# Column sums of phi(k) by a DMA transpose, a VectorE sum and a broadcast read of a DRAM row, in place of a matmul with ones

## Chip, cores and metric

One core of a Trainium2 chip. The metric is the device time of one execution in microseconds. The kernel before takes 213.39 us (median of 6 runs, 212.61 to 214.76).

## The reference, cut to what matters

A linear-attention block and a SwiGLU block on the same normed input, added to the residual. S = 2048 rows, D = 512, 32 heads of 16, F = 1792.

```python
pq, pk = phi(q), phi(k)
kv = jnp.einsum("bhsd,bhse->bhde", pk, v)
z = jnp.einsum("bhsd->bhd", pk)                      # the column sums: 512 numbers
num = jnp.einsum("bhqd,bhde->bhqe", pq, kv)
den = jnp.einsum("bhqd,bhd->bhq", pq, z)[..., None] + 1e-6
o = num / den
...
return x + _A_ref(xn, A_wqkv, A_wo) + _B_ref(xn, B_w_gate, B_w_up, B_w_down)
```

Only z is in question: pk summed over all 2048 rows, then needed in every partition, since den multiplies it by pq row by row.

## The kernel before

Rows lie on partitions. GpSimd and VectorE add the 16 tiles of pk into two accumulators; zb is their sum, 128 partitions x 512. What is left is a sum over the 128 partitions whose result must stand in all of them. A matmul with a matrix of ones does both at once.

```python
NGU = NCH * NFC                                       # 56 gate/up blocks, j = 0..55
O_SLOT = {4: 0, 7: 1, 10: 2, 13: 3}                   # block of a group of 14 -> output tile
PZ_AT = {9 + 11 * t // 4: t for t in range(16)}       # block after which tile t is multiplied by z
DIV_AT = {j + 1: t for j, t in PZ_AT.items()}         # one block later it is divided
...
        def z_bf():      # VectorE
            zb = zacc[0] + zacc[1]
        def z_mm():
            K.add("pe", lambda e: e.matmul(banks[3][:, :], ones[:, :], zb[:, :], start=True, stop=True), ...)
            K.add("act", lambda e: e.activation(zbc[:, :], banks[3][:, :], ACT.Copy), ...)
        def pz_mul(t):   # GpSimd: pz = pq[t] * zbc
        def divide(t):   # VectorE: den = sum over 16 of pz; reciprocal; pq[t] *= 1/den; then a DMA transpose of pq[t]
...
        for j in range(NGU):
            gu(j)        # TensorE: 4 gate and 4 up matmuls of 128x512, banks 4..7 in turn; ScalarE: silu of the gate
            hop(j)       # VectorE: hT = up * silu(gate); frees the up bank for block j + 2
            ...
            if j in DIV_AT: divide(DIV_AT[j])
            if j in PZ_AT:  pz_mul(PZ_AT[j])
            if C >= 1 and fc in O_SLOT: otile(4 * (C - 1) + O_SLOT[fc])
```

(Shortened, with cuts at "...".) VectorE runs its instructions in program order; on VectorE the divide of a tile stands between the hops of two blocks; and the up matmuls of block j + 2 write the bank that hop(j) frees.

Of the kernel before, what the change touches and what calls it, by code (L numbers as in the profile page):

```python
# [6 lines left out]
ACT = mybir.ActivationFunctionType  # L7
ALU = mybir.AluOpType

P = 128  # L10
S = 2048
D = 512
# [3 lines left out]
NG = D // P  # L16
# [6 lines left out]

CENTRED = (0, 1)
NWARM = 8
O_SLOT = {4: 0, 7: 1, 10: 2, 13: 3}
PZ_AT = {9 + 11 * t // 4: t for t in range(16)}
DIV_AT = {j + 1: t for j, t in PZ_AT.items()}


# [77 lines left out]
def bass_parallel_sum__linear_attn_block__swiglu_ffn__prompt_kernel(nc, A_x, A_wqkv, A_wo, B_x, B_w_gate, B_w_up, B_w_down, out):  # L108
    xin = A_x[0]
    oview = out[0]  # L110
    K = _Program()
    bf, f32 = dt.bfloat16, dt.float32

    with contextlib.ExitStack() as es:
        E = es.enter_context

        def sb(name, shape, dtype):
            return E(nc.sbuf_tensor(name, shape, dtype))
# [20 lines left out]
        zb = sb("zb", [P, D], bf)  # L139
# [4 lines left out]
        zbc = sb("zbc", [P, D], f32)  # L144
# [3 lines left out]
        sil = sb("sil", [P, 2, 512], bf)  # L148
        out_sb = sb("out_sb", [P, 2, D], bf)
        ident = sb("ident", [P, P], bf)  # L150
        ones = sb("ones", [P, P], bf)
        maskt = sb("maskt", [P, P], bf)
        eps5 = sb("eps5", [P, 1], f32)
        stats = sb("stats", [P, NT, 6], f32)
# [16 lines left out]
        banks = [E(nc.psum_tensor("pb%d" % i, [P, 512], f32)) for i in range(8)]  # L171

        def B(i):
            return ("bank", i)
# [48 lines left out]
        for t in range(4, 16):  # L223
# [5 lines left out]
            out=ident[:, :], in_=ident[:, :], compare_op=ALU.not_equal, fill=1.0,  # L229
            base=0, pattern=[[-1, P]], channel_multiplier=1), r=[("ident",)], w=[("ident",)])  # L230

        def blockmask(key, ap, view, pat):
            K.add("pool", lambda e: e.memset(ap, 1.0), w=[key])
            K.add("pool", lambda e: e.affine_select(
                out=view, in_=view, compare_op=ALU.is_ge, fill=0.0, base=0,
                pattern=[[-DH, HPG]] + pat, channel_multiplier=1), r=[key], w=[key])
            K.add("pool", lambda e: e.affine_select(
                out=view, in_=view, compare_op=ALU.is_ge, fill=0.0, base=DH - 1,
                pattern=[[DH, HPG]] + pat, channel_multiplier=-1), r=[key], w=[key])

        blockmask(("maskt",), maskt[:, :], maskt[:, :].rearrange("p (a b) -> p a b", a=HPG), [[0, DH]])
        K.add("pool", lambda e: e.memset(ones[:, :], 1.0), w=[("ones",)])

        def keep_busy(k, n):
            one = nc.const_aps.tensor(1.0, (P, 512), bf)
# [200 lines left out]
        def z_add(half, i):  # L446
            acc, key = zacc[:, half, :], ("zacc", half)
            t = NZP * half + i
            if half == 0 and i == 1:
                K.add("pool", lambda e: e.tensor_scalar(  # L450
                    out=acc, in0=pk[:, 0, :], scalar1=rstd[:, 0:1], scalar2=0.0, op0=ALU.mult, op1=ALU.add),
                    r=[("pk", 0), ("rs", 0)], w=[key])
                K.add("pool", lambda e: e.tensor_scalar(
                    out=zt, in0=pk[:, 1, :], scalar1=rstd[:, 1:2], scalar2=0.0, op0=ALU.mult, op1=ALU.add),
                    r=[("pk", 1), ("rs", 1)], w=[("pz", 0)])
                K.add("pool", lambda e: e.tensor_tensor(out=acc, in0=acc, in1=zt, op=ALU.add),
                      r=[key, ("pz", 0)], w=[key])
                return
            first, fkey = (pk[:, t - 1, :], ("pk", t - 1)) if i == 1 else (acc, key)
            K.add("dve" if half else "pool",  # L460
                  lambda e: e.tensor_tensor(out=acc, in0=first, in1=pk[:, t, :], op=ALU.add),  # L461
                  r=[fkey, ("pk", t)], w=[key])
# [50 lines left out]
        def gu(j, extra=(), er=(), ew=()):  # L513
            C, fc = j // NFC, j % NFC
            n = (len(extra) + 7) // 8
            todo = list(extra)
            for b, w_, key in ((gb(j), wg, "wg"), (gb(j) + 1, wu, "wu")):
                fns = []
                for c in range(NDC):
                    fns.append(lambda e, c=c, b=b, w_=w_: e.matmul(  # L520
                        banks[b][:, :], w_[:, c, fc * P:(fc + 1) * P], xnT[:, c, C * 512:(C + 1) * 512],
                        start=(c == 0), stop=(c == NDC - 1)))
                    fns += todo[:n]
                    todo = todo[n:]
                K.add("pe", fns,
                      r=sum([xkeys(t) for t in range(4 * C, 4 * C + 4)], []) + [(key, fc // 7)] + list(er),
                      w=[B(b)] + list(ew))
            K.add("act", lambda e: e.activation(sil[:, j % 2, :], banks[gb(j)][:, :], ACT.Silu),  # L528
                  r=[B(gb(j))], w=[("sil", j % 2)])

        def hop(j):
            C, fc = j // NFC, j % NFC
            K.add("dve", lambda e: e.tensor_tensor(  # L533
                out=hT[:, C % 2, fc, :], in0=banks[gb(j) + 1][:, :], in1=sil[:, j % 2, :], op=ALU.mult),
                r=[B(gb(j) + 1), ("sil", j % 2)], w=[("hT", C % 2, fc)] + (shared.get((C, fc), []) if C < 2 else []))
# [8 lines left out]
        def kv_fns():  # L544
            return [(lambda e, c=c, g=g: e.matmul(  # L545
                banks[0][:, g * P:(g + 1) * P], wqkv[:, c, 2 * D + g * P:2 * D + (g + 1) * P],
                GT[:, c, g * P:(g + 1) * P], start=(c == 0), stop=(c == NDC - 1)))
                for g in range(NG) for c in range(NDC)]

        def kv_mask():  # L550
            K.add("dve", lambda e: e.tensor_tensor(
                out=kvT[:, :, :], in0=banks[0][:, :].rearrange("p (g e) -> p g e", g=NG),
                in1=maskt[:, :][:, None, :].broadcast_to([P, NG, P]), op=ALU.mult),
                r=[B(0), ("maskt",)], w=[("kvT",)])

        def z_bf():
            K.add("dve", lambda e: e.tensor_tensor(out=zb[:, :], in0=zacc[:, 0, :], in1=zacc[:, 1, :], op=ALU.add),
                  r=[("zacc", 0), ("zacc", 1)], w=[("zb",)])

        def z_mm():  # L560
            K.add("pe", lambda e: e.matmul(banks[3][:, :], ones[:, :], zb[:, :], start=True, stop=True),
                  r=[("zb",), ("ones",)], w=[B(3)])
            K.add("act", lambda e: e.activation(zbc[:, :], banks[3][:, :], ACT.Copy), r=[B(3)], w=[("zbc",)])

        def heads(ap):
            return ap.rearrange("p (h d) -> p h d", d=DH)
# [2 lines left out]
        def pz_mul(t):  # L569
            K.add("pool", lambda e: e.tensor_tensor(out=pz[:, t % 2, :], in0=pq[:, t, :], in1=zbc[:, :], op=ALU.mult),  # L570
                  r=[("pq", t), ("zbc",)], w=[("pz", t % 2)])
# [25 lines left out]
        def m_mm(g):  # L597
            K.add("pe", lambda e: e.matmul(banks[MB[g]][:, :], kvT[:, g, :], wo[:, g, :], start=True, stop=True),  # L598
                  r=[("kvT",), ("wo", 0)], w=[B(MB[g])])
            K.add("act", lambda e: e.activation(M[:, g, :], banks[MB[g]][:, :], ACT.Copy), r=[B(MB[g])], w=[("M", g)])  # L600
# [19 lines left out]
        def otile(t):  # L620
            b = t % 4
            ogroup(b, t, 0, D)
            oout(b, t, 0, D)
# [7 lines left out]
        for j in range(NGU):  # L631
            C, fc = j // NFC, j % NFC
            if j == 2:
                gu(j, kv_fns(), [("GT", c) for c in range(NDC)] + [("wqkv", 2, 0)], [B(0)])
            else:
                gu(j)
            hop(j)
            if j == 1:
                z_add(1, 1)
            elif j == 2:  # L640
                kv_mask()
                z_add(1, 2)
            elif j == 3:
                z_add(1, 3)
            elif j == 4:
                m_mm(0)
                m_mm(1)
                z_add(1, 4)
            elif j == 5:
                m_mm(2)  # L650
                m_mm(3)
                z_add(1, 5)
            elif j == 6:
                z_bf()
            elif j == 8:
                z_mm()
            if j in DIV_AT:
                divide(DIV_AT[j])
            if j in PZ_AT:
                pz_mul(PZ_AT[j])  # L660
            if C >= 1 and fc in O_SLOT:
                otile(4 * (C - 1) + O_SLOT[fc])
        for t in range(12, 15):
# [42 lines left out]
```

## Time and profile before

| | before |
|---|---|
| time, median of 6 | 213.39 us |
| span of the profiled execution | 211.8 us |
| TensorE busy | 208.0 us |
| TensorE waiting for another engine after 60 us | 0.2 us of weight load |

### The profile page before, as it was taken

What the parts mean: (1) busy time and instruction counts of PE and PEld (TensorE: products, weight loads), DVE (VectorE), ACT (ScalarE), POOL (GpSimd) and SP (SyncE); (2) the same over time, 40 slices, a digit from 0 to 9 for tenths busy, and PEclk for the clock granted to TensorE, in tenths of its full rate; (3) what the DMA queues carried; (4) which work ended last, traced back from release to release, by engine and by line L of the source; (5) the groups of instructions that cost most, each with busy time, mean ns of one, the idle gap of its engine ahead of it and who ended that gap; (6) DMA issues with size and microseconds to landing.
All of it is one profiled execution on the core that took longest, in us unless ns stands there. A gap on an engine that the chain in (4) does not pass through costs nothing.

```text
span 211.8 us, 2736 instructions
## 1 busy us (share of the span) xinstructions
PE 208.0 (98%) x1009; PEld 95.7 (45%) x1009; DVE 129.2 (61%) x224; ACT 70.3 (33%) x146; POOL 62.9 (30%) x92
## 2 busy tenths in 40 slices
PE   8899899999999999999999999999999999999996
PEld 2344344444544444444444444444444444444455
DVE  3898988973864788654654775564639463542122
ACT  4989886406364333122131313021223122130000
POOL 3879877899402322210201220220204000000000
PEclk9999999999999999999999999999999999999999
DMA  6954731399920021102101011101011101100101
GB/s 177 353 139 101 72 73 35 63 387 370 357 88 0 3 50 25 50 0 53 25 25 25 25 29 50 25 25 50 8 44 26 50 7 46 25 25 0 49 25 53
DMA packets 27997, 16.04 MB, mean 76 GB/s; under 512 B 17872, under 2 KB 27984, under 8 KB 27984
## 3 DMA queue, kind: packets, MB, share of 16 engines
q1 hardware_dynamic: 27152, 15.15, 26.3%
q10 hardware_dynamic: 832, 0.72, 1.1%
q8 instruction: 8, 0.13, 0.3%
q14 instruction: 5, 0.04, 0.1%
HBM read 9.70 MB, written 2.10 MB: 56 GB/s over the span
## 4 chain that ended last, share of the span: by engine, by line
PE 90%; DVE 4%; DMA 3%; POOL 1%; SPq 1%; ACT 1%; issue 0%
PE pb L520 46%; PE pb L608 23%; PE pb L389 7%; PE pb L604 7%; PE pb L438 6%; DMA x_sb<-in_A_x_dram 3%; DVE pk L428 1%; SPq L178 1%; DVE pq L428 1%; DVE stats L256 1%; POOL ef L417 1%; ACT ef L410 1%; PE pb L545 0%; PE pb L598 0%; POOL xn L344 0%
## 5 line engine op out<-in xcount | busy, mean ns | idle before, releaser
L528 ACT ACTIVATE sil<-pb 128x512 bf16<-128x512 f32 x56 | 33.3, 597 | 101.2 <-PE pb L520 98.8
L533 DVE TENSOR_TENSOR hT<-pb,sil 128x512 bf16<-128x512 f32 x56 | 38.1, 687 | 36.7 <-PE pb L520 33.8
L520 PE MATMUL pb<-xnT,wg 128*128 128x512 bf16 x224 | 57.8, 379 | 0.0
L520 PE MATMUL pb<-xnT,wu 128*128 128x512 bf16 x224 | 57.8, 379 | 0.0
L608 PE MATMUL pb<-wd,hT 128*128 128x512 bf16 (+2 forms) x252 | 51.4, 355 | 0.0
L570 POOL TENSOR_TENSOR pz<-pq,zbc 128x512 f32<-128x512 bf16 x16 | 18.6, 1163 | 90.5 <-DVE den L575 78.5
L608 PEld LDWEIGHTS pb<-wd,hT 128*128 128x128 bf16 x252 | 23.5, 98 | 25.0
L520 PEld LDWEIGHTS pb<-xnT,wu 128*128 128x128 bf16 x224 | 21.9, 98 | 25.9 <-DVE hT L533 0.2
L520 PEld LDWEIGHTS pb<-xnT,wg 128*128 128x128 bf16 x224 | 21.9, 98 | 25.8
L614 DVE TENSOR_TENSOR out_sb<-pb,x_sb 128x512 bf16<-128x512 f32 (+2 forms) x18 | 11.4, 632 | 33.2 <-PE pb L608 33.2
L389 PE MATMUL pb<-wqkv,xnT 128*128 128x512 bf16 x112 | 25.2, 379 | 0.8 <-DVE pq L428 0.6
L587 DVE TENSOR_TENSOR pq<-pq,rden 128x512 bf16<-128x512 bf16 x16 | 17.5, 1094 | 0.6
L389 PEld LDWEIGHTS pb<-wqkv,xnT 128*128 128x128 bf16 x112 | 10.8, 98 | 14.5 <-DVE pq L428 1.4
L417 POOL TENSOR_SCALAR ef<-ef 128x512 bf16<-128x512 bf16 x25 | 15.8, 634 | 5.0 <-ACT ef L410 4.5
L604 PE MATMUL pb<-M,pk 128*128 128x512 bf16 (+2 forms) x72 | 16.8, 355 | 0.0
L410 ACT ACTIVATE ef<-pb 128x512 bf16<-128x512 f32 x25 | 14.7, 591 | 3.8 <-PE pb L389 3.8
L256 DVE BATCH_NORM_STATS2 stats<-x_sb 128x6 f32<-128x512 bf16 x16 | 10.9, 679 | 3.6 <-DMA x_sb<-in_A_x_dram 3.6
L438 PE MATMUL pb<-pk,xn 128*128 128x512 bf16 x56 | 12.7, 379 | 0.0
L575 DVE TENSOR_REDUCE den<-pz 128x32 f32<-128x512 f32 x16 | 10.8, 675 | 0.0
L428 DVE SCALAR_TENSOR_TENSOR pk<-pb,ef 128x512 bf16<-128x512 f32 x14 | 9.6, 685 | 1.8 <-POOL ef L417 1.6
L461 POOL TENSOR_TENSOR zacc<-zacc,pk 128x512 f32<-128x512 f32 x8 | 10.2, 1279 | 0.6
L604 PEld LDWEIGHTS pb<-M,pk 128*128 128x128 bf16 x72 | 6.8, 98 | 7.4
(77 smaller groups left out, 109.8 us busy)
## 6 DMA issues: line engine op xcount, KB each, us to landing
out_dram<-out_sb SPq DMA_DIRECT2D x15, 128.0 KB, 1.7
x_sb<-in_A_x_dram SPq DMA_DIRECT2D x14, 128.0 KB, 4.5
wg<-in_B_w_gate_dram SPq DMA_DIRECT2D x2, 896.0 KB, 8.3
wu<-in_B_w_up_dram SPq DMA_DIRECT2D x2, 896.0 KB, 9.7
wd<-in_B_w_down_dram SPq DMA_DIRECT2D x2, 896.0 KB, 13.9
wqkv<-in_A_wqkv_dram ACTq DMA_DIRECT2D x2, 256.0 KB, 4.7
wqkv<-in_A_wqkv_dram SPq DMA_DIRECT2D x2, 256.0 KB, 5.0
wqkv<-in_A_wqkv_dram SPq DMA_DIRECT2D x1, 512.0 KB, 7.8
```

The source lines that it names most:

```text
L389: K.add("pe", [(lambda e, c=c: e.matmul(banks[b][:, :], src[:, c, t * P:(t + 1) * P], wqkv[:, c, col:col + D], start=(c == 0), stop=(c == ...
L410: K.add("act", lambda e: e.activation(buf, banks[b][:, :], ACT.Exp), r=[B(b)], w=[bkey])
L417: K.add("pool", lambda e: e.tensor_scalar(out=buf, in0=buf, scalar1=top, scalar2=0.0, op0=ALU.min, op1=ALU.max), r=[bkey] + tkeys, w=[bkey])
L428: K.add("dve", lambda e: e.scalar_tensor_tensor(out=dst, in0=val, scalar=low, in1=mid, op0=ALU.max, op1=ALU.add), r=keys + lkeys, w=[dkey])
L438: K.add("pe", [(lambda e, c=c: e.matmul(banks[c][:, :], src[:, t, c * P:(c + 1) * P], pk[:, t, :], start=first, stop=last)) for c in range ...
L520: fns.append(lambda e, c=c, b=b, w_=w_: e.matmul(banks[b][:, :], w_[:, c, fc * P:(fc + 1) * P], xnT[:, c, C * 512:(C + 1) * 512], start=(c ...
L528: K.add("act", lambda e: e.activation(sil[:, j % 2, :], banks[gb(j)][:, :], ACT.Silu), r=[B(gb(j))], w=[("sil", j % 2)])
L533: K.add("dve", lambda e: e.tensor_tensor(out=hT[:, C % 2, fc, :], in0=banks[gb(j) + 1][:, :], in1=sil[:, j % 2, :], op=ALU.mult), r=[B(gb( ...
L570: K.add("pool", lambda e: e.tensor_tensor(out=pz[:, t % 2, :], in0=pq[:, t, :], in1=zbc[:, :], op=ALU.mult), r=[("pq", t), ("zbc",)], w=[( ...
L587: K.add("dve", lambda e: e.tensor_tensor(out=heads(pq[:, t, :]), in0=heads(pq[:, t, :]), in1=rden[:, i, :][:, :, None].broadcast_to([P, NH ...
L604: fns = [(lambda e, g=g: e.matmul(banks[bank][:, 0:hi - lo], pk[:, t, g * P:(g + 1) * P], M[:, g, lo:hi], start=(g == 0), stop=False)) for ...
L608: fns = [(lambda e, fc=fc: e.matmul(banks[bank][:, 0:hi - lo], hT[:, C % 2, fc, jj * P:(jj + 1) * P], wd[:, fc, lo:hi], start=False, stop= ...
```

## The change

Its intent is to take the sum off TensorE and PSUM: the DMA engine turns zb so that columns lie on partitions, VectorE sums along the free dimension, and the 512 sums go through a row in DRAM, which is read back into all partitions. As the way is longer, the multiplies and divides start three blocks later and three of four output tiles one block later.

```diff
-O_SLOT = {4: 0, 7: 1, 10: 2, 13: 3}
-PZ_AT = {9 + 11 * t // 4: t for t in range(16)}
+O_SLOT = {5: 0, 8: 1, 11: 2, 13: 3}
+PZ_AT = {12 + 11 * t // 4: t for t in range(16)}
...
+        zrow = nc.dram_tensor("zrow", [1, D], f32, kind="Internal").ap()
...
-        def z_mm():
-            K.add("pe", lambda e: e.matmul(banks[3][:, :], ones[:, :], zb[:, :], start=True, stop=True), ...
-            K.add("act", lambda e: e.activation(zbc[:, :], banks[3][:, :], ACT.Copy), ...
+        def z_turn():      # after z_bf, block 6
+            K.add("sp", lambda e: e.dma_start_transpose(out=zT[:, :, :], in_=zb[:, :]), ...
+        def z_sum():       # block 8
+            K.add("dve", lambda e: e.tensor_reduce(
+                out=zc[:, :], in_=zT[:, :, :], axis=mybir.AxisListType.X, op=ALU.add), ...
+            K.add("sp", lambda e: e.dma_start(zrow[0].rearrange("(g p) -> p g", g=NG), zc[:, :],
+                                            allow_slow_non_contiguous=True), ...
+            K.add("sp", lambda e: e.dma_start(zbc[:, :], zrow.broadcast_to([P, D])), ...
```

(The memset of ones goes too; operand lists are cut.)

More of the change, by code (lines that the diff above doesn't have):

```diff
@@ L150, in bass_parallel_sum__linear_attn_block__swiglu_ffn__prompt_kernel @@
         ident = sb("ident", [P, P], bf)
-        ones = sb("ones", [P, P], bf)
+        zT = sb("zT", [P, NG, P], bf)
+        zc = sb("zc", [P, NG], f32)
+        zrow = nc.dram_tensor("zrow", [1, D], f32, kind="Internal").ap()
         maskt = sb("maskt", [P, P], bf)
@@ L241, in bass_parallel_sum__linear_attn_block__swiglu_ffn__prompt_kernel @@
         blockmask(("maskt",), maskt[:, :], maskt[:, :].rearrange("p (a b) -> p a b", a=HPG), [[0, DH]])
-        K.add("pool", lambda e: e.memset(ones[:, :], 1.0), w=[("ones",)])
         def keep_busy(k, n):
@@ L558, in z_bf @@
                   r=[("zacc", 0), ("zacc", 1)], w=[("zb",)])
-        def z_mm():
-            K.add("pe", lambda e: e.matmul(banks[3][:, :], ones[:, :], zb[:, :], start=True, stop=True),
-                  r=[("zb",), ("ones",)], w=[B(3)])
-            K.add("act", lambda e: e.activation(zbc[:, :], banks[3][:, :], ACT.Copy), r=[B(3)], w=[("zbc",)])
+        def z_turn():
+            K.add("sp", lambda e: e.dma_start_transpose(out=zT[:, :, :], in_=zb[:, :]), r=[("zb",)], w=[("zT",)], dma=True)
+        def z_sum():
+            K.add("dve", lambda e: e.tensor_reduce(
+                out=zc[:, :], in_=zT[:, :, :], axis=mybir.AxisListType.X, op=ALU.add), r=[("zT",)], w=[("zc",)])
+            K.add("sp", lambda e: e.dma_start(zrow[0].rearrange("(g p) -> p g", g=NG), zc[:, :],
+                                            allow_slow_non_contiguous=True),
+                  r=[("zc",)], w=[("zrow",)], dma=True)
+            K.add("sp", lambda e: e.dma_start(zbc[:, :], zrow.broadcast_to([P, D])),
+                  r=[("zrow",)], w=[("zbc",)], dma=True)
         def heads(ap):
@@ L654, in bass_parallel_sum__linear_attn_block__swiglu_ffn__prompt_kernel @@
                 z_bf()
+                z_turn()
             elif j == 8:
-                z_mm()
+                z_sum()
             if j in DIV_AT:
```

## The prediction

> **What bounds the kernel now.** I read the page first, then the chain of waits in order of time, the list of waits, and the timeline around the sum.
>
> The busy shares and the chain, from the page:
>
> ```profile
> PE 208.0 (98%) x1009; PEld 95.7 (45%) x1009; DVE 129.2 (61%) x224; ACT 70.3 (33%) x146; POOL 62.9 (30%) x92
> ...
> PE 90%; DVE 4%; DMA 3%; POOL 1%; SPq 1%; ACT 1%; issue 0%
> PE pb L520 46%; PE pb L608 23%; PE pb L389 7%; PE pb L604 7%; PE pb L438 6%; DMA x_sb<-in_A_x_dram 3%; DVE pk L428 1%; SPq L178 1%; DVE pq L428 1%; DVE stats L256 1%; POOL ef L417 1%; ACT ef L410 1%; PE pb L545 0%; PE pb L598 0%; POOL xn L344 0%
> ```
>
> TensorE is the bound: 90% of the span lies on its instructions in the chain. In order of time the chain stays on TensorE without a break from 25.60 to 210.02 us, so from there on only two things move the end: matmul work put in or taken out, and a wait that stops TensorE. The piece that the change takes out stands in that chain:
>
> ```profile
> 61.19 5.18 PE pb L520 x24
> 66.37 0.22 PE pb L561
> 66.58 17.27 PE pb L520 x80
> 83.85 0.86 PE pb L604 x4
> ```
>
> So the matmul with ones (L561) is worth 0.22 us of the path, and between it and the first output tile at 83.85 us TensorE only does gate and up matmuls, which do not need the sum.
>
> The waits from 60 us on show who is close to TensorE and who is not:
>
> ```profile
> POOL pz L570 <- DVE den L575: 78.5, 14, 7.9
> POOL pz L570 <- ACT zbc L563: 12.0, 1, 12.0
> ...
> PEld pb L520 <- DVE hT L533: 0.2, 1, 0.2
> ```
>
> GpSimd, the consumer of the broadcast row zbc, is idle most of the time. The only wait of TensorE is 0.2 us of weight load on VectorE's hop (the product that frees an up bank). This matters: VectorE runs in order, and where it stands still the hop comes late and TensorE stops two blocks later.
>
> VectorE's timeline where the row is made and first used:
>
> ```profile
> 63.63 0.68 DVE L557 TENSOR_TENSOR zb<-zacc 128x512 bf16<-128x512 f32 x1
> 64.75 0.69 DVE L533 TENSOR_TENSOR hT<-pb,sil 128x512 bf16<-128x512 f32 x1 [0.44 <-PE pb L520]
> 66.47 0.69 DVE L533 TENSOR_TENSOR hT<-pb,sil 128x512 bf16<-128x512 f32 x1 [1.03 <-PE pb L520]
> 68.42 0.69 DVE L533 TENSOR_TENSOR hT<-pb,sil 128x512 bf16<-128x512 f32 x1 [1.25 <-PE pb L520]
> 70.14 0.69 DVE L533 TENSOR_TENSOR hT<-pb,sil 128x512 bf16<-128x512 f32 x1 [1.03 <-PE pb L520]
> 70.75 0.68 DVE L575 TENSOR_REDUCE den<-pz 128x32 f32<-128x512 f32 x1
> ```
>
> zb is ready at 64.31. zbc stood ready at 67.22 (the ACT copy L563, 66.62 + 0.60), and its first user, the divide of tile 0, began at 70.75.
>
> **What the Trainium skill says.** "DMA: Bandwidth & Descriptors", section "Rules for kernel authors": a strided last dimension becomes one descriptor per element, so the store of the 512 sums is 512 pieces of 4 bytes; the trace of before has no such store, but it has transposes that move as many small packets (474 under 512 B in the window of one of them), and these land in 2.4 us. The same page, "Anatomy of one DMA": a DMA has a fixed cost near 2 us (fitted for the GpSimd path), most of it the receipt of the write, heaviest for HBM; the trace agrees roughly for these queues, 1.5 us for a 32 KB store to DRAM and 2.1 us for a 64 KB load. The same page, "Two DMAs through the same engine are not ordered": a DMA that reads what another wrote must wait for its completion. The issue order of the changed kernel has this wait, so the two fixed costs add up. "VectorE: DVE Perf Modes", "The perf-mode tier table": tensor_reduce has only the 1x form whatever the type. The trace has 0.675 us for 512 f32 a partition (L575), so I take 0.68 for 512 bf16.
>
> **The change part by part.**
>
> Removed: one 128x512 matmul, 0.22 us on the path; its ACT copy, 0.60 us, beside other work (ACT is 33% busy); one memset on GpSimd at the start, off the path.
>
> Added: a DMA transpose of zb, one VectorE reduce (0.68 us), a store of 2 KB in 512 pieces, and a load of that row into 128 partitions (256 KB). The DMA queues are empty then: the window view has 0 GB/s from 63.0 to 66.3 us, the weights having landed.
>
> Moved: the 16 multiplies and divides go three blocks later (the divide of tile 0 from block 10 to block 13, the last from 51 to 54), and output tiles 0, 1 and 2 of each group one block later. A block is 8 matmuls, 1.73 us. TensorE's amount of work is the same but for the 0.22.
>
> The new path to zbc, step by step:
> - zb ready 64.31. The transpose is issued at 64.34 (the queue has only waited) and lands after 2.4 (the median of the transposes of pq): 66.75.
> - The reduce stands on VectorE behind the hop of block 8, which ends at 67.16, so it does not wait for the transpose: 67.16 to 67.84. The next hop is due at 68.42 - 0.22 = 68.20, so it is not delayed.
> - The store: issued 67.87; by a transpose's 2.4 us it lands at 70.3. A plain 32 KB store takes 1.5; I take the larger for the 512 pieces.
> - The broadcast load: between 2.1 us (64 KB) and 4.7 us (256 KB while 350 GB/s of other loads run). Scaling from the first, 192 KB more at some 350 GB/s are 0.55 us: 2.7. zbc at about 73.0.
>
> When it is needed: the hop of block 10 started at 70.14, so that of block 13 starts at 70.14 + 3 x 1.726 - 0.22 = 75.10, and the divide 0.61 later, at 75.71. The multiply before it takes 1.16 on GpSimd, so zbc may land at 74.5 with nobody waiting. The two divides close together (blocks 13 and 15, as 10 and 12 before) gave that 0.2 us wait of the weight load; so VectorE may slip some 0.15 us more before TensorE stands. TensorE therefore stops for max(0, landing - 74.65). With 73.0 that is 0, a margin of 1.6 us.
>
> The later end: the last divide goes to block 54. In the tail TensorE still has the output tiles 11 to 14 ahead of tile 15, 4 x 3.88 = 15.5 us, while divide and transpose need about 2.0 + 2.4. Divides and output tiles now never share a block (before, 18, 21 and 32 did), and every tile's divide still lies at least six blocks ahead of the tile's use (tile 0: block 13 against 19, tile 3: 21 against 27). So no new wait there.
>
> Sum: -0.22 + 0 = -0.2 us of 213.42, giving 213.2.
>
> **The rivals.**
>
> First rival: the chain of DMAs is slower than its parts, and the divide waits for zbc. Two of its steps have no twin in the trace, the 4-byte store into DRAM and the broadcast load. For it: the skill warns of such stores, and 2.4 + 2.7 is estimated, not read. If each took 4.5 us, zbc would land at 76.9 and TensorE would stop 2.2 us once: 215.4, 1% slower, still "same". For 2% (4.3 us) the two would have to take 5.6 us each. Against it: the queue is empty and the sizes are small. The wait would come once, since the blocks after it move along.
>
> Second rival: VectorE becomes the bound by the moved divides, one more hop late in each group. For it: VectorE's in-order queue is what TensorE waits for first. Against: it is 61% busy, the divides keep their spacing of two and three blocks, and output tiles of 3.88 us now lie behind several of them, in which VectorE catches up. I would give it 0 to 0.5 us.
>
> Third rival: it is faster by more than the matmul, since ACT and a PSUM bank are freed. Against: no wait of TensorE in the list names ACT or bank 3 after 25 us. At most 0.3 us, 213.1.
>
> **Range and chances.** The kernel before itself ran between 212.61 and 214.76, so the range is that of the runs with a little of the first rival on top: 212.3 to 215.0. Faster by over 2% would need 4.3 us from a part worth 0.22: 1%. Slower by over 2% needs the first rival at more than twice my estimate for both transfers: 3%. Within 2%: 96%. Predicted 213.2.
>
> **What would show it.** In the profile after: L561 gone and no new wait of PE above 0.3 us between 60 and 80 us; the zT transpose landing near 66.8 and the reduce starting at 67.2 right behind a hop; the store landing in about 2.4 us and the broadcast in 2.7; the first multiply on GpSimd at 72 to 74.5 instead of 67.30; the divide of tile 0 at 75.7 with no idle time for GpSimd before it. The prediction is wrong if zbc lands after 74.7 and VectorE sits idle before the first den reduce for GpSimd, followed by a gap in PE of that size near 79 us, or if the span of TensorE's work grows elsewhere, in particular by repeated waits on the hop after divides.

## More of the kernel before

The span is cut into 40 slices of 5.3 us; a digit is tenths, of busy time for PE and of full clock for PEclk. TensorE is busy from end to end and its clock is never lowered:

```profile
PE   8899899999999999999999999999999999999996
...
PEclk9999999999999999999999999999999999999999
```

## The result, and the profile after

The changed kernel takes 221.49 us (median of 6 runs, 220.41 to 222.5) against 213.39 (6 runs). The ratio is 1.0376, 95% interval 1.033 to 1.0421: 3.8% slower. A ratio here and below is the mean time of one kernel's fast runs over that of the other's in the same rounds, so not quite the ratio of the medians.

The page of the changed kernel, busy shares, slices and chain:

```profile
PE 211.4 (96%) x1008; PEld 97.0 (44%) x1008; DVE 129.8 (59%) x225; ACT 69.9 (32%) x145; POOL 62.7 (28%) x91
...
PE   8899999999999944999999999999999999999996
...
PEclk9999999999999996799999999999999999999999
...
PE 81%; DMA 9%; DVE 5%; POOL 2%; SPq 1%; issue 1%; ACT 1%; DVEq 0%
```

Three things to see. There is a hole in the PE row at slices 15 and 16. PEclk falls to 0.6 and 0.7 just there and in the slice after. And TensorE has one matmul fewer (1008 for 1009) but 3.4 us more busy time: the same work has run slower.

The chain in order of time (start, length, what) walks through the hole:

```profile
61.67 5.19 PE pb L521 x24
...
67.65 0.60 DVE zc L566
68.27 8.30 DMA zrow<-zc
76.58 4.69 DMA zbc<-zrow
...
81.34 1.17 POOL pz L579
...
85.20 0.69 DVE hT L534
...
85.94 9.04 PE pb L521 x28
```

The chain leaves TensorE for the sum, its store (8.30 us) and its broadcast read (4.69 us), then the first multiply on GpSimd, the divide and the hop on VectorE, and only then comes back to TensorE. The 28 matmuls after it take 9.04 us; at 0.216 us each, the pace before, they would take 6.05. The length of a DMA here, and in all that follows, runs from its issue until it has landed, that is, until its completion is signalled.

The record of DMA packets shows where in the store's 8.30 us the time lies. The row is the stretch from 68 to 78 us in 40 slices of 0.25 us, a digit the busy share of the 16 DMA engines in tenths; the line under it gives packets, MB and share:

```profile
DMA  0000180000009000000000000000000000000000
...
q1 hardware_dynamic: 528, 0.00, 2.5%
```

All 528 packets of the store (its 512 pieces and 16 more) lie in the two slices from 69.0 to 69.5 us. (The 9 at 71 us is one packet of the instruction queue.) So some 7 of the 8.30 us pass after the last recorded packet, and the trace does not show what happens in them.

The waits give the same from each engine's side:

```profile
POOL pz L579 <- DMA zbc<-zrow: 25.6, 1, 25.6
...
DVE den L584 <- POOL pz L579: 6.2, 1, 6.2
PE pb L521 <- DVE hT L534: 6.1, 1, 6.1
```

GpSimd's 25.6 us are harmless in themselves. But VectorE has run into its divide and waits 6.2 us for GpSimd there, with two hops queued behind it, and so TensorE stands 6.1 us before the up matmuls of block 16.

Finally the stretches of the hole: length, then busy time and instructions of PE, PEld, DVE, ACT and POOL, then the granted clock, DMA share and GB/s.

```profile
66.70:79.60 12.90, 12.90 (x61) 5.77 (x59) 4.74 (x7) 4.18 (x7) 0.00 (x0) 1.00 0.06 5
79.60:86.00 6.40, 0.27 (x2) 0.07 (x2) 3.36 (x6) 0.02 (x1) 3.39 (x3) 0.91 0.16 34
86.00:92.00 6.00, 6.00 (x15) 2.13 (x16) 4.02 (x7) 1.17 (x2) 1.17 (x1) 0.53 0.22 44
92.00:95.00 3.00, 3.00 (x15) 1.37 (x14) 1.61 (x5) 1.19 (x2) 0.28 (x1) 1.00 0.00 0
```

For 6 us after the hole the clock is 0.53; then it is 1.00 again.

The sum for the two profiled executions (211.8 to 221.2, +9.4): TensorE stands 6.1; the 28 slow matmuls cost 9.04 - 6.05 = 3.0; the matmul with ones is gone, -0.2; and the unbroken chain on TensorE starts at 26.09 for 25.60, +0.5, on the first loads of x and not on anything the change touches. That makes 9.4. The profiled execution is the slowest of the six, which is why the medians differ by 8.1 only.

### The profile page after: what moved, and what is told of

The parts are those of the page before. It is cut to its first block, busy times and chain, and to the rows that moved or that the text cites. A ratio compares the mean times of both kernels' runs of the same rounds, so it can differ in the third digit from the quotient of the medians.

```text
span 221.2 us, 2736 instructions
## 1 busy us (share of the span) xinstructions
PE 211.4 (96%) x1008; PEld 97.0 (44%) x1008; DVE 129.8 (59%) x225; ACT 69.9 (32%) x145; POOL 62.7 (28%) x91
## 4 chain that ended last, share of the span: by engine, by line
PE 81%; DMA 9%; DVE 5%; POOL 2%; SPq 1%; issue 1%; ACT 1%; DVEq 0%
PE pb L521 39%; PE pb L617 22%; PE pb L390 7%; PE pb L613 6%; PE pb L439 6%; DMA zrow<-zc 4%; DMA x_sb<-in_A_x_dram 3%; DMA zbc<-zrow 2%; DVE pk L429 1%; SPq L180 1%; DVE pq L429 1%; DVE stats L257 1%; DVE hT L534 1%; POOL ef L418 1%; POOL pz L579 1%
## 5 line engine op out<-in xcount | busy, mean ns | idle before, releaser
L521 PE MATMUL pb<-xnT,wu 128*128 128x512 bf16 x224 | 59.6, 388 | 6.1 <-DVE hT L534 6.1
L521 PE MATMUL pb<-xnT,wg 128*128 128x512 bf16 x224 | 59.0, 385 | 0.0
```

The lines of the kernel that those rows point to most:

```text
L521: fns.append(lambda e, c=c, b=b, w_=w_: e.matmul(banks[b][:, :], w_[:, c, fc * P:(fc + 1) * P], xnT[:, c, C * 512:(C + 1) * 512], start=(c ...
```

## The experiments

Theory A, formed from this: the moved schedule is free and the removed matmul is worth its 0.2 us; everything lost comes from the row landing after its need, as a standstill of TensorE plus a few microseconds of lowered clock after it. Rival B: the moved divides and output tiles cost part of it. Within A it was open why the store takes 8.3 us and whether the slow matmuls are the clock or VectorE's backlog.

**sched_only: the move without the DMAs.** The matmul with ones is kept.

```diff
 # kernel before
-O_SLOT = {4: 0, 7: 1, 10: 2, 13: 3}
-PZ_AT = {9 + 11 * t // 4: t for t in range(16)}
+O_SLOT = {5: 0, 8: 1, 11: 2, 13: 3}
+PZ_AT = {12 + 11 * t // 4: t for t in range(16)}
```

> The kernel before, with the matmul with ones kept, and only the multiplies, divides and output tiles moved as the change moves them. Theory A (the late row alone costs): within 0.5% of the kernel before, 213.4 us, TensorE clock 1.0. Rival B (the moved schedule costs part of the 8 us): 215 or more.

Measured: 213.36 us against 213.49, ratio 1.0004 (0.9985 to 1.0022), clock 1.0. Rival B is out.

**dma_early: the DMAs without the move.** The changed kernel with the two lines of the kernel before.

```diff
 # changed kernel
-O_SLOT = {5: 0, 8: 1, 11: 2, 13: 3}
-PZ_AT = {12 + 11 * t // 4: t for t in range(16)}
+O_SLOT = {4: 0, 7: 1, 10: 2, 13: 3}
+PZ_AT = {9 + 11 * t // 4: t for t in range(16)}
```

> The changed kernel with the schedule of the kernel before (first multiply at block 9 and not 12). Theory A: the row still lands near 81, the deadline moves 3 blocks = 5.2 us earlier, so TensorE stands about 11.3 us instead of 6.1 and loses the same 3 us to the lower clock: 221.5 + 5.2 = 226.7. Rival B: no later than the changed kernel, since the moved schedule is undone.

Measured: 227.15 us, ratio 1.0641 (1.0622 to 1.066), clock 0.97. The waits show the longer stand:

```profile
PE pb L521 <- DVE hT L534: 11.8, 1, 11.8
```

So the move does not cost time; it saves about 5.7 us, where theory A has 5.2 for three blocks.

**probe: the DMAs by themselves.** A small kernel that issues one DMA at a time on an idle chip, each when the one before has landed, and each twice. Its output is wrong, which doesn't matter for the time.

> The DMAs alone, one after the other on an idle chip, each issued when the one before has landed, twice each (the output is wrong on purpose; it only copies x). Theory 1, each 4-byte piece costs its engine a round trip of its own (32 pieces an engine, (8.3 - 1.5)/32 = 0.21 us each): the store as in the changed kernel lands in about 8 us; the same 512 pieces 512 bytes apart take the same 8; 128 pieces of 4 bytes take 1.5 + 8 x 0.21 = 3.2; 128 pieces of 16 bytes 3.2; 512 pieces of 64 bytes still about 8. Theory 2, pieces that share a line of DRAM stand in each other's way: 512 bytes apart they land in about 2.4 us, 512 pieces of 64 bytes in about 2.4 as well. Theory 3, it is the number of pieces and not DRAM: the same 512 pieces written into 128 partitions of SBUF take 8 too; if DRAM is the cause these take about 2. Broadcast load: as in the changed kernel 4.7 us; if reading one row 128 times is what costs, the plain load of 128 rows of 2 KB takes under 3.

Landing times, from the list of DMA issues (name, count, KB, median us to landing; d_p is the one with 16-byte pieces, t the one into SBUF, and the d_q of 32 KB the one with 64-byte pieces):

```profile
bc<-d_asis SPq DMA_DIRECT2D x2, 256.0 KB, 3.2
pl<-d_q SPq DMA_DIRECT2D x2, 256.0 KB, 2.6
...
d_q<-s SPq DMA_DIRECT2D x2, 32.0 KB, 1.8
d_asis<-s SPq DMA_DIRECT2D x2, 2.0 KB, 9.1
d_wide<-s SPq DMA_DIRECT2D x2, 2.0 KB, 2.4
d_p<-s SPq DMA_DIRECT2D x2, 2.0 KB, 1.5
d_one<-s SPq DMA_DIRECT2D x2, 0.5 KB, 8.0
t<-s SPq DMA_DIRECT2D x2, 2.0 KB, 2.0
```

The number of pieces is not it: 512 pieces of 4 bytes placed 512 bytes apart (d_wide) land in 2.4 us, and a quarter of the pieces side by side (d_one, 128) still take 8.0. Theory 1 is wrong. The packets agree: those of d_one (8.0 us) and of d_p (1.5 us) are all recorded by about 1.0 us after the issue, so what differs is only the time from the last packet to the landing. Nor is it small pieces as such: into SBUF 512 of them take 2.0. What is slow is many small pieces side by side in DRAM, theory 2. The broadcast read takes 3.2 us, where 4.7 was expected, for 2.6 of a plain load of the same size.

**probe_step and probe_line: what has to be shared.** The same method (outputs wrong again).

> More DMAs alone, one after the other, twice each (the output is wrong on purpose). The first probe showed 128 pieces of 4 bytes side by side at 8.0 us, 512 pieces of 4 bytes 512 bytes apart at 2.4, 128 pieces of 16 bytes side by side at 1.5. Theory 2a, the cost is that pieces of different DMA engines meet in one line of DRAM[...]: at 16 bytes from piece to piece four partitions fill a line of 64 bytes, so a step of 4 or 2 words decides: with a line of 64 bytes, steps of 1 and 2 words are slow (8 us), 4, 8 and 16 words fast (1.5 to 2); with a line of 32 bytes 2 words is fast already. Pairs of words (8 bytes side by side) go as the step of 2 words does. Theory 2b, it is pieces under 16 bytes that share a line, whoever writes them: 4 words (16 bytes, 4 pieces a line) and 8 words are slow as well. If the cost is a fixed one, 32, 8 and 2 partitions of 4 bytes take 8 us too where more than one engine writes the line; if it adds up piece by piece they take 1.5 + a quarter, a sixteenth of the 6.5. Last, store and broadcast load in turn: if the load right after a slow store is slowed by it, bc takes 4.7 as in the changed kernel and bcb, after the quick store, about 3.2.

> DMAs alone again, twice each (wrong output on purpose), to tell what is shared when the 4-byte store is slow. The step probe gave 8.5 us for pieces one word apart, 3.6 two words apart, 1.6 four words apart (one piece in each 16 bytes). Two readings are left. Lines and engines: a piece waits for pieces that another engine writes into its 64-byte line. Then four words apart but begun 32 bytes into a line (d_fourby), where each line holds pieces of two groups of four partitions, is as slow as two words apart, about 3.6, while the one begun at a line (d_fourat) stays at 1.6; the 16-byte pieces likewise (d_quadby 3.2 against d_quadat 1.5); and four 4-byte pieces of one partition side by side (d_own, 512 pieces, each line from one group) are quick, about 2. Words: only pieces that share 16 or 32 bytes disturb each other, whoever writes them. Then d_fourby and d_quadby stay near 1.5, and d_own is slow, 8 or more. d_twoat and d_oneat repeat 3.6 and 8.5.

Stores of 128 partitions unless noted, median of two. The two of a pair can lie far apart: side by side 7.3 to 9.5 us, with 32 partitions 3.1 and 5.7.

| pieces | spacing in DRAM | lands after, us |
|---|---|---|
| 4 bytes | 4 bytes, side by side | 8.5; 8.4 in the other run |
| 4 bytes | 8 bytes | 3.6; 3.3 |
| 8 bytes | side by side | 3.2 |
| 4 bytes | 16 bytes, from the start of the tensor | 1.6; 1.7 |
| 4 bytes | 16 bytes, begun 32 bytes later | 2.6 |
| 4 bytes | 32 bytes | 1.8 |
| 4 bytes | 64 bytes | 1.4 |
| 16 bytes | side by side | 1.7 |
| 16 bytes | side by side, begun 32 bytes later | 1.8 |
| 4 bytes, four from each partition | side by side (d_own) | 7.5 |
| 4 bytes, 32 partitions only | side by side | 4.4 |

What follows: the time rises as pieces lie closer; at 16 bytes from piece to piece it is down to 1.6 to 2.6 us. The reading with DMA engines meeting in a line is wrong as it was put (it takes for granted that neighbouring partitions share an engine and that tensors begin at a line, which no run here shows): d_own, where each partition fills its own 16 bytes, should have been quick by it and takes 7.5. The reading with words of 16 or 32 bytes is right for d_own and d_quadby, but not for the 2.6 of d_fourby. And 32 partitions took 3.1 and 5.7 us; 8 and 2 partitions left no landing time in the list, but the next DMA could be issued about 1.1 us later. So the cost is not a fixed one; the two values for 32 are too far apart to tell whether it adds up piece by piece. The exact rule stays open; that it is made by pieces under 16 bytes lying close together in DRAM is shown. The last part found no slowing of the broadcast read by a slow store ahead of it: 3.8 us after the slow one, 4.1 after the quick one.

**piece16: the same change with 16-byte pieces.** zb's columns are permuted as it is written, so that after the transpose partition p holds the sums 4p to 4p + 3 and the store is contiguous. The result stays right.

```diff
 # changed kernel
-            K.add("dve", lambda e: e.tensor_tensor(out=zb[:, :], in0=zacc[:, 0, :], in1=zacc[:, 1, :], op=ALU.add),
+            K.add("dve", lambda e: e.tensor_tensor(out=zb[:, :].rearrange("p (g c) -> p c g", g=NG),
+                in0=zacc[:, 0, :].rearrange("p (c g) -> p c g", g=NG),
+                in1=zacc[:, 1, :].rearrange("p (c g) -> p c g", g=NG), op=ALU.add),
...
-            K.add("sp", lambda e: e.dma_start(zrow[0].rearrange("(g p) -> p g", g=NG), zc[:, :],
+            K.add("sp", lambda e: e.dma_start(zrow[0].rearrange("(p g) -> p g", g=NG), zc[:, :],
```

> The changed kernel with zb's columns permuted as it is written, so that the store is 128 pieces of 16 bytes, contiguous in DRAM; the result stays right. By theory 1 of the probe the store lands in about 3.2 to 3.7 us instead of 8.3, zbc 4.6 to 5 us earlier, near 76.5. TensorE stands about 1.3 to 1.8 us. If the lower clock follows only from a long gap, it stays at 1.0 and the time is about 215; if any gap costs it, about 218. If the 4-byte pieces were not the cause of the 8.3 us, 221.5 as before.

Measured: 212.67 us against 213.49, ratio 0.9968 (0.9945 to 0.9991), clock 1.0. The two DMAs, and the permuted add:

```profile
zbc<-zrow SPq DMA_DIRECT2D x1, 256.0 KB, 3.8
...
zrow<-zc SPq DMA_DIRECT2D x1, 2.0 KB, 1.6
```

```profile
63.00 2.43 DVE L558 TENSOR_TENSOR zb<-zacc 128x512 bf16<-128x512 f32 x1
```

The store lands in 1.6 us, better than the 3.2 to 3.7 that theory 1 gave, and the row is in time though the permuted add takes 2.43 us for 0.68. With the layout of one store changed, the whole 8 us are back. This is the test that settles the cause inside the kernel; that it is the layout and not the number of pieces, which falls from 512 to 128 as well, is shown by the probe (128 pieces of 4 bytes side by side: 8.0).

**busy_gap: is it the clock?** Work is put in the hole.

```diff
 # changed kernel, in gu(j), between the gate and the up matmuls
+                if j == 16 and key == "wu":
+                    K.add("pe", [(lambda e: e.matmul(banks[3][:, :], xnT[:, 0, 0:P], xnT[:, 0, 0:512], start=True, stop=True))
+                                 for _ in range(28)], r=xkeys(0), w=[B(3)])
```

> The changed kernel with 28 matmuls of 128x512 on data at hand, written to a free bank and never read, put where TensorE stands (between the gate and up matmuls of block 16): 28 x 0.216 = 6.05 us of work in a gap of 6.1. Theory A (some 3 us of the loss are the lower clock that follows the gap): the clock stays at 1.0 and the time falls by 3, to 218.6. Rival (the slow blocks after the gap are VectorE's backlog of divides, not the clock): 221.5 as before.

Measured: 219.78 us, ratio 1.0302 (1.0268 to 1.0335), clock 1.0 in all four runs.

```profile
78.64 6.21 PE L527 MATMUL pb<-xnT 128*128 128x512 bf16 x28
86.12 1.04 PE L521 MATMUL pb<-xnT,wu 128*128 128x512 bf16 x4 [1.27 <-DVE hT L537]
...
92.31 1.03 PE L616 MATMUL pb<-M,pk 128*128 128x512 bf16 x4
```

The 28 matmuls from 86.12 to the output tile at 92.31 now take 6.19 us, for 9.04 in the changed kernel, beside the same divides. So the lowered clock is what made them slow, not VectorE. The total is 1.2 over the expected 218.6: in this run store and read took 9.0 and 5.2 us, 1.2 more than in the changed kernel's profile, and a stand of 1.3 was left. With 28 useless matmuls more the kernel takes 1.7 us less, though in other rounds, and the intervals of the two ratios just meet (1.0335 and 1.033).

**start14 and start17: later still.** The row as slow as before, its first use two and five blocks later.

```diff
 # changed kernel; start14
-PZ_AT = {12 + 11 * t // 4: t for t in range(16)}
+PZ_AT = {14 + 21 * t // 8: t for t in range(16)}
 # start17
-O_SLOT = {5: 0, 8: 1, 11: 2, 13: 3}
-PZ_AT = {12 + 11 * t // 4: t for t in range(16)}
+O_SLOT = {8: 0, 10: 1, 12: 2, 13: 3}
+PZ_AT = {17 + 5 * t // 2: t for t in range(16)}
```

(The words cut from the next expectation gave a length for the gap; it is the Trainium skill's, cited in the section on the prediction.)

> The changed kernel with the first multiply two blocks later (14 and not 12; every 2.625 blocks instead of 2.75 so that the last still fits). The deadline moves 2 x 1.73 = 3.45 us: TensorE stands 6.1 - 3.45 = 2.65. If the lower clock needs a gap[...]: clock 1.0 and 213.2 + 2.65 = 215.9. If any gap of this kind costs the clock: about 218.8.

Measured: 218.03 us (216.63 to 218.95), ratio 1.0208 (1.0165 to 1.0251), so that it is not told from 2%. The stand was 3.65 us in the profiled run and not 2.65, as store and read took 8.9 and 5.0. It seems to lie on the edge of what lowers the clock: the profiled run kept 1.0 and took 216.63, the other three had a mean clock of 0.992 and took 217.8 to 218.95, 1.2 to 2.3 us more.

> The changed kernel with the first multiply five blocks later (17; then every 2.5 blocks; output tiles at 8, 10, 12, 13). The deadline moves 8.6 us, past the row's landing. Theory A: no gap, clock 1.0, 213.2 us with the slow store still there and still over 8 us. If the DMAs cost something besides the late row: over 214.

Measured: 212.86 us against 213.41, ratio 0.9966 (0.9946 to 0.9986), clock 1.0. No wait of TensorE is in its list after 60 us, although its store took 8.9 us and its read 5.1:

```profile
zbc<-zrow SPq DMA_DIRECT2D x1, 256.0 KB, 5.1
...
zrow<-zc SPq DMA_DIRECT2D x1, 2.0 KB, 8.9
```

GpSimd starts at 81.84, and the first divide only at 84.28. So the slow DMAs by themselves cost nothing. Lateness costs.

**piece16_14: both remedies.** The permuted store and the first multiply at block 14.

> The 16-byte store and the multiplies two blocks later still (start at block 14): the row lands 2 us or more ahead of its need, and the two short waits of the weight load on VectorE's hop that the 16-byte kernel had (1.0 us in the list, some 0.3 us of TensorE) should shrink to the 0.2 of the kernel before. Theory A: 212.4 to 212.7 us, 0.3% under the kernel before by the matmul left out (0.22) and little else; not told from the 16-byte kernel's 212.67. Above 213.5 would mean that the DMAs cost TensorE in another way than by lateness.

Measured: 212.94 us against 213.31, ratio 0.9979 (0.9955 to 1.0003); no wait of TensorE after 60 us is left. That is a little over the expected 212.4 to 212.7. It is not told from piece16 or start17. Those two are 0.3% under the kernel before, and no run here gained more; whether the part of it beyond the matmul's 0.22 us is real was not settled.

## Why the prediction was wrong

Its text has the right mechanism as the first rival, with 3% for what happened. By its own steps:

- *TensorE is the bound, the matmul is worth 0.22, the moved schedule costs nothing.* Right: sched_only 1.0004, and start17 and piece16 at or a little under the kernel before.
- *zb, transpose, sum.* Right: transpose 2.4 us as predicted, sum 0.67 us, straight behind a hop.
- *The store, 2.4 us.* Wrong, and the step that failed. It landed in 8.30. The twin chosen for it was the transpose, "as many small packets"; but this tells only what the number of pieces costs. For that it was even right: 512 pieces of 4 bytes 512 bytes apart take 2.4. The mistake was to leave out where they land. In the row they lie side by side, and there 128 suffice for 8.0.
- *The broadcast read, 2.7 us.* Too small: 4.69 in the kernel. Reading one row 128 times takes 3.2 alone for 2.6 of a plain load; the rest, seen in every profile here with the slow store (4.7 to 5.2), less with the quick one (3.8 and 4.1), lies before the read's first packet: that is recorded 2.6 us after the issue in the changed kernel and 1.0 in the probe, and from there both take 2.1 to 2.2. What holds it back was not tested.
- *When the row is needed, 74.65.* Right. In the changed kernel's time, 0.5 later, it is 75.1; the row landed at 81.27; the difference is 6.1, and TensorE stood 6.13.
- *"TensorE therefore stops for max(0, landing - 74.65)."* Incomplete. The formula prices a stand at its own length. The 28 matmuls after it cost 3.0 us more, and busy_gap shows that this is the clock. The Trainium skill states this in "TensorE: Matmul & The Clock Gate", section "HAM oscillation — how this bites in real kernels": "no PE-idle gaps >~3.4µs", else the clock falls to half. The trace agrees: 0.53 after 6.1 us, full clock after 1.3, and 3.65 us at the edge. This page was not used for the prediction, since it foresaw no gap. It should have been, for the rival: an estimate from the page's 3.4 us of sustained work at half clock is 1.7 us on top of any stand that long (3.0 were measured after 6.1), so a stand of some 3.4 us, and not of 4.3, would have been seen to pass the 2%.
- *The chances.* The rival needed store and read at 5.6 each to lose 2%; they took 13.0 together. The two steps "estimated, not read" were named as the weak ones, and then given hardly any of the weight. The small number of bytes and the empty queue, the arguments against, had no bearing on what made the store slow. A warning stood in the diff, allow_slow_non_contiguous, but it does not tell a slow store from a quick one: piece16 has it too and lands in 1.6. The skill's "DMA: Bandwidth & Descriptors", section "Specifications", has transfers under 512 bytes done by read-modify-write; no run here shows whether that is so, but small size alone is not dear (1.4 to 2.6 us for 4-byte pieces at least 16 bytes apart), only close company is.

## What to carry to other kernels

Look at where the pieces of a store meet in DRAM, not only at how many there are: choose the layout on the compute side so that each partition writes 16 contiguous bytes or more, the smallest piece tried here that was quick side by side (1.4 to 1.8 us). Where a slow transfer feeds an in-order engine that also frees the bound engine's buffers, the number that counts is the margin between landing and need, and here moving the first use by five blocks did as much as a faster store. When that margin is overdrawn, price a long TensorE stand with time at half clock on top: 3.0 us after the stand of 6.1 here, and 1.2 to 2.3 us more in the three runs of start14 that lost some clock (profiled stand 3.65).

## What the Trainium skill lacked or had wrong

- "DMA: Bandwidth & Descriptors" gives stores with a strided last dimension as one piece per element, and transfers under 512 bytes as read-modify-write. It lacks that pieces close together in DRAM are far dearer than the same pieces apart: 128 pieces of 4 bytes take 8.0 to 8.5 us side by side, 3.3 to 3.6 at 8 bytes, 1.6 to 1.7 at 16 bytes (2.6 where they begin 32 bytes later); 512 of them take 9.1 to 10.3 side by side and 2.4 at 512 bytes; pieces of 16 bytes side by side take 1.4 to 1.8.
- The same page lacks what a broadcast read of one DRAM row costs: 256 KB from a row of 2 KB took 3.2 to 4.1 us alone and 3.8 to 5.2 in the kernels, where a plain load of 256 KB took 2.6.
- "TensorE: Matmul & The Clock Gate" agrees in its threshold: the kernel with a profiled stand of 3.65 us kept the clock in that run and lost some of it in its other three; the one with 6.1 us lost it in all six. After the stand of 6.1 it stayed at half for some 6 us of work. The page has about 3.4 us of sustained work to regain it, but in a window that runs free of the kernel, so this is no contradiction; here it cost 3.0 us.
- "VectorE: DVE Perf Modes" has no cost for an add whose result is written in a permuted order (neighbouring results 256 bytes apart): 2.43 us for 128x512 f32 into bf16, against 0.68 in plain order. "SBUF — State Buffer" has a penalty for accesses that leave a line of 16 bytes, but no time for it.
